# A spectral-mixing kernel on one core: features folded as well as tokens, with rows turned round through memory on ScalarE's queue

## The chip, the cores and the metric

The kernel runs on one core of a Trainium2 chip. The metric is the device time of one execution in microseconds (us); less is better. The five engines of a core are named as in the profile: PE (TensorE: matmuls, transposes; PEld is its weight load), DVE (VectorE), ACT (ScalarE), POOL (GpSimd) and SP (SyncE, which here only issues DMAs). Each engine works through its own instructions in a fixed order and waits for other engines and for DMAs by semaphores. All times of before are from one profiled execution unless a line says otherwise.

## The reference

Attention with a sigmoid in the place of a softmax, a real 2D Fourier transform with a residual, a layer norm and a feed-forward block with a second residual, in float32 on 8 batches of 448 tokens with 12 heads of 64 (768 features):

```python
scores = matmul(q, k.transpose(0, 1, 3, 2)) / sqrt(64) - log(448)
attn = matmul(1 / (1 + exp(-scores)), v)
x = attn.transpose(0, 2, 1, 3).reshape(8, 448, 768)

mixed = real(fft(fft(x, axis=1), axis=2))       # over tokens, then over features
u = x + mixed
mu = mean(u, -1); var = mean((u - mu) ** 2, -1)
un = (u - mu) / sqrt(var + 1e-6)
y = u + maximum(un @ w_ch1, 0) @ w_ch2          # 768 -> 3072 -> 768
```

## The kernel before

**Phases.** The first quarter of the span (to about 381 us) is attention and mixing, batch by batch. While it runs, the FFN's weights are read, split and combined in the background (`weight`, line 287: ACT L305, DVE L310 to L319, one weight block after another, with buffers `wr`, `wt`). After it the FFN runs: first token chunk 0 by plain products (PE `psh` L607 and `po` L627, while ACT, DVE and POOL make the weights for the fast form, L456, L458, L466), then the other chunks by a fast scheme (`psf` L845, `pso` L901).

**The attention loop.** The loop over `t` (line 567) goes in steps of two, one step being about 1.96 us on PE; 8 steps make a group of 4 heads and 24 steps a batch. In each pass PE makes scores (L139, L152), ACT the sigmoid `a` (L127) and the upper part `hi` of the next queries and keys (L115), DVE their remainder `lo` (L123), and PE the products with the values (`av`, L165 and L177), which ACT copies out as `xT` (L185): features on the partitions, 6 blocks of 128, and tokens along the row, folded already by even and odd halves (2 x 225). What else runs at a step is written down by hand with `at(t, fn)`; `pin` (line 503) then fixes each engine's order as emitted, so nothing is reordered later. An instruction that waits holds up all behind it on its engine.

**Mixing.** The transform over features is a matmul with cosines and sines (`stage_d`, PE `psd` L216), that over tokens a second one (`stage_s`, PE `pss` L227). Ahead of both, POOL folds `xT`: per feature pair p of three, sums and differences of blocks p and p+3 (`eo`, L197), then of even and odd token halves (`fd`, L200), then of tokens mirrored (`xp`, L203); 6 operations each, 18 per batch, in three rounds at steps 12 to 17, 20 to 25, and 28 and 29 of the batch (table FOLDS, line 32). `stage_d` is then 24 matmuls of 193 columns per batch (2 x 2 outputs, 2 parities, 3 pairs). ACT copies the result to `A` (L220); `stage_s` is 4 matmuls of 385 columns, with a copy `Q` on ACT (L231) and sum and difference `sm`, `df` on DVE (L236). PE transposes `xT` back (`psx`, L248), DVE adds (`u`, L255), SP stores `u` to `u_dram` (L263).

These units of batch b come in three chunks (`mix_some`, line 485), each ahead of a new group of heads: chunk 1 at step 24b+36 (two `psd` outputs, the first `pss`), chunk 2 at 24b+44 (the other two `psd`, three transposes), chunk 3 at 24b+52, which is step 28 of the next batch (two `pss`, the other five transposes). PE runs a chunk in one piece, so it waits there for ACT's `A` and `Q` and for DVE's `df` and `u`; a `u` also frees the PSUM bank that a later `pss`, `psx` or `av` needs. The units of the last batch run later, among the first products of the FFN (`mix_rest`, line 654).

**First norms.** The norm of chunk 0 (512 tokens, two groups of two 128-row tiles) is spread over steps too (`norm_plan`, line 430). From a group's start: load `un` at +4, statistics (DVE L373, L376) at +10, the inverse root by some ten tiny DVE operations on `mv` (L382 to L394) at +11, scaling `un` (DVE L399) at +17, the fp16 upper half `hl` (ACT L422) at +19 and +27, its remainder (DVE L426) and two transposing DMAs `ut<-hl` at +22 and +30. The groups start at steps 96 and 128.

Of the kernel before, what the change touches and what calls it, by code (L numbers as in the profile page):

```python
# [9 lines left out]
F32 = mybir.dt.float32  # L10
# [41 lines left out]
def spectral_attention_ffn(tc, qk, v, w1, w2, cd, cs, ident_in, out):  # L52
# [8 lines left out]
    with ExitStack() as top:  # L61
# [19 lines left out]
        if True:  # L81
# [87 lines left out]
            def values(gg, w):  # L169
                b, r = divmod(gg, NG)  # L170
                p = r + 3 * w
                vr, ps = vrs[gg], avs[gg][w]
                for c in range(3):
                    a = att.pop((2 * gg + w, c))
                    for j in range(2):
                        h = c * 256 + (2 * w + j) * D
                        nc.tensor.matmul(  # L177
                            ps[j * D:(j + 1) * D, :SQ], vr[:, h:h + D], a[:, j], start=False, stop=(c == 2))
# [6 lines left out]
                nc.scalar.activation(xT[:, p].rearrange("d r k -> d (r k)"), ps[:, :SQ], AF.Copy)  # L185

            eos = {}

            def fold(b, p, n, e):

                xT, xp = xts[b]
                lv, n = divmod(n, 2)
                op = (ALU.add, ALU.subtract)[n]
                if lv == 0:
                    if n == 0:
                        eos[p] = [fx.tile([128, 2, 2, HS], F32, tag=t, name=t) for t in ("eo", "fd")]
                    e.tensor_tensor(out=eos[p][0][:, n], in0=xT[:, p], in1=xT[:, p + 3], op=op)  # L197
                elif lv == 1:
                    eo, fd = eos[p]
                    e.tensor_tensor(out=fd[:, n], in0=eo[:, :, 0], in1=eo[:, :, 1], op=op)  # L200
                else:
                    fd = eos[p][1]
                    e.tensor_tensor(  # L203
                        out=xp[:, n, :, :, p], in0=fd[:, :, :, 0:HM], in1=fd[:, :, :, HS - 1:HM - 2:-1], op=op)

            def mix_units(b):
                xT, xp = xts[b]
                A = fx.tile([HM, 2, 2, 386], F32, tag="A", name="A")
                ps_d, sd, ut = {}, {}, {}

                def stage_d(kp, c, par, p):
                    m = HM - kp
                    if par == 0 and p == 0:
                        ps_d[c, kp] = ps_m.tile([128, 512], F32, tag="m", name="psd")
                    ps = ps_d[c, kp]
                    nc.tensor.matmul(  # L216
                        ps[:HM, par * 193:par * 193 + 193], xp[:, kp ^ c, c, par, p],
                        cd_sb[:, c, par, p], start=(p == 0), stop=(p == 2))
                    if par == 1 and p == 2:
                        act_next.append(lambda: nc.scalar.activation(  # L220
                            A[:, kp, c].rearrange("s (i r) -> s r i", r=2),
                            ps[:HM, 0:386].rearrange("s (r i) -> s r i", r=2), AF.Copy))

                def stage_s(kp, c):
                    m = HM - kp
                    ps = ps_m.tile([128, 512], F32, tag="m", name="pss")
                    nc.tensor.matmul(  # L227
                        ps[:m, :385], cs_sb[:HM, kp, c, :m], A[:, kp, c, :385], start=True, stop=True)
                    if c == 1:
                        sd["Q", kp] = Q = fx.tile([128, 385], F32, tag="Q", name="Q", bufs=2)  # L230
                        act_next.append(lambda: nc.scalar.activation(Q[:m], ps[:m, :385], AF.Copy))  # L231
                    else:
                        Q = sd["Q", kp]
                        sd[kp] = [fx.tile([128, 385], F32, tag=n, name=n) for n in ("sm", "df")]
                        for o, op in zip(sd[kp], (ALU.add, ALU.subtract)):
                            dve_next.append(lambda o=o, op=op: nc.vector.tensor_tensor(  # L236
                                out=o[:m], in0=ps[:m, :385], in1=Q[:m], op=op))

                def add_x(kp, r, hf):
# [6 lines left out]
                    ps = ps_m.tile([128, 512], F32, tag="m", name="psx")  # L246
                    for i in range(3):
                        nc.tensor.transpose(  # L248
                            ps[:HM - kp, i * 128:(i + 1) * 128], xT[:, hf * 3 + i, r, kp:HS:2], ident)
                    y = d if hf == r else s  # L250
                    m = HM - kp
                    ysl = y[:m, 384:0:-1] if hf else y[:m, 0:384]

                    def add():
                        nc.vector.tensor_tensor(  # L255
                            out=u[:m, hf * 384:hf * 384 + 384], in0=ps[:m, :384], in1=ysl, op=ALU.add)
                        if hf:
# [10 lines left out]
                def units_d(kp, c):  # L268
                    return [(0.33, lambda par=par, p=p: stage_d(kp, c, par, p)) for par in range(2) for p in range(3)]

# [58 lines left out]
            def weight_row():  # L329
# [3 lines left out]
                top = cpool.tile([128, 1], F32, name="top")  # L333
                row = cpool.tile([128, 128], F32, name="row")
                nc.vector.tensor_reduce(out=top[:2], in_=ps[:2, :128], op=ALU.max, axis=AX.X)
# [693 lines left out]
def _layout(q, k, v, w1, w2):  # L1029
    import numpy as np  # L1030
    B = q.shape[0]

    qt, kt = (a.reshape(B, 2, NG, 2, S, D).transpose(0, 2, 1, 3, 5, 4).reshape(B, 2 * NG, 2 * D, S) for a in (q, k))
# [60 lines left out]
```

## Time and profile before

| | |
|---|---|
| median of 3 runs | 1582.52 us (1581.5 to 1583.43) |
| the profiled execution's own time | 1581.96 us |
| its span (first to last instruction) | 1580.2 us |
| PE busy | 99% of the span |
| DVE busy | 81% |
| ACT busy | 42% |
| POOL busy | 20% |

The profile lists groups of instructions by source line. `out<-in` are the tiles written and read, followed by their shapes; `xN` is a count; then come busy time, the mean duration in ns, and idle time of that engine just before the group with whatever released it. A row of a timeline is: start in us, time taken, engine, line, operation, tiles, count, and in brackets the idle time before it and its releaser. A row of a table of stretches has the stretch (from:to), its length, and the busy time of PE, PEld, DVE, ACT and POOL with their instructions (x), the granted clock of PE (1.00 is full), the busy share of the 16 DMA engines, and GB/s.

### The profile page before, as it was taken

How to read it: one execution, taken by the hardware profiler on the slowest of the kernel's cores; microseconds unless marked ns; L12 is line 12 of the kernel's file. 1: busy time of each engine (PE TensorE's matmuls, PEld its weight loads, DVE VectorE, ACT ScalarE, POOL GpSimd, SP SyncE). 2: the span in 40 equal slices, each digit the busy share in tenths (PEclk: the TensorE clock that was granted, in tenths of full speed). 3: DMA queues.
4: the chain of work that ended last, by engine and by line, in shares of the span. 5: the costliest groups of instructions: out<-in, count | busy, mean ns of one | idle time of the engine just before them, and what ended most of it. 6: DMA issues, size and time to landing. Idle time of an engine off the chain costs nothing.

```text
span 1580.2 us, 27410 instructions
## 1 busy us (share of the span) xinstructions
PE 1557.3 (99%) x11059; PEld 1064.9 (67%) x11059; DVE 1277.1 (81%) x2354; ACT 656.4 (42%) x780; POOL 322.5 (20%) x244
## 2 busy tenths in 40 slices
PE   8999999899999999999999999999999999999998
PEld 3556565466555567777777777777777777777775
DVE  4997788794699946887888888888788878887778
ACT  7777777665555424222232233232423233223221
POOL 3644343355788810000000000000000000000000
PEclk9999999999999999999999999999999999999999
DMA  7888878783788977668667766866776777576571
GB/s 291 313 313 277 308 260 304 258 298 107 287 278 292 320 306 293 199 234 306 234 191 289 253 235 227 306 205 252 259 255 195 282 288 234 168 298 259 195 273 49
DMA packets 130399, 402.43 MB, mean 255 GB/s; under 512 B 68832, under 2 KB 70112, under 8 KB 111712
## 3 DMA queue, kind: packets, MB, share of 16 engines
q1 hardware_dynamic: 130272, 400.68, 71.1%
q8 instruction: 86, 1.41, 0.4%
q14 instruction: 41, 0.34, 0.1%
HBM read 311.39 MB, written 73.92 MB: 244 GB/s over the span
## 4 chain that ended last, share of the span: by engine, by line
PE 72%; DVE 3%; ACT 1%; issue 0%; DVEq 0%; ACTq 0%
PE pso L901 30%; PE psf L845 30%; PE psh L607 6%; PE po L627 5%; DVE F L851 1%; PE psd L216 0%; DVE H L851 0%; ACT H L880 0%; DVE ur L648 0%; DVE ur L929 0%; DVE acc L978 0%; DVE acc L916 0%; PE psx L248 0%; ACT F L870 0%; DVE X L851 0%
## 5 line engine op out<-in xcount | busy, mean ns | idle before, releaser
L845 PE MATMUL psf<-ut,ws 128*128 128x256 f16 x4536 | 506.6, 273 | 1.2 <-DVE ur L648 1.2
L901 PE MATMUL pso<-ws,H 128*128 128x384 f16 x3024 | 503.4, 326 | 1.1 <-DVE H L851 0.9
L845 PEld LDWEIGHTS <-ws 128*128 128x128 f16 x4536 | 443.6, 98 | 60.6 <-issue 1.7
L901 PEld LDWEIGHTS <-H 128*128 128x128 f16 x3024 | 295.5, 98 | 190.0 <-DVE H L851 1.7
L870 ACT ACTIVATE F<-F 128x1024 f32<-128x1024 f32 x72 | 76.1, 1057 | 406.5 <-DVE F L851 406.5
L916 DVE TENSOR_TENSOR acc<-pso,acc 128x384 f32<-128x384 f32 x399 | 207.9, 551 | 19.7 <-PE pso L901 19.7
L851 DVE TENSOR_TENSOR H<-F,H 128x1024 f16<-128x1024 f32 (+1 forms) x144 | 155.4, 1088 | 48.8 <-ACT H L880 48.5
L880 ACT ACTIVATE H<-F 128x1792 f16<-128x1792 f32 x72 | 122.2, 1697 | 110.7 <-DVE F L851 110.7
L127 ACT ACTIVATE a<-sc 128x900 f32<-128x900 f32 x168 | 147.2, 920 | 48.4 <-PE sc L139 47.7
L851 DVE TENSOR_TENSOR F<-X,psf 128x256 f32<-128x256 f32 x288 | 117.2, 419 | 59.3 <-PE psf L845 54.7
L466 POOL TENSOR_TENSOR wq<-wq 128x384 f32<-128x384 f32 x96 | 152.0, 1589 | 31.4 <-DVE wp L458 25.8
L851 DVE TENSOR_TENSOR F<-F 128x256 f32<-128x256 f32 x288 | 109.5, 422 | 24.8 <-ACT F L870 20.1
L177 PE MATMUL av<-a,vr 128*64 128x450 f32 x576 | 119.1, 550 | 0.0
L458 DVE SCALAR_TENSOR_TENSOR wp<-wq,wsc,wp 128x1536 f16<-128x1536 f32 x48 | 98.2, 2076 | 17.3 <-ACT wp L456 17.3
L851 DVE TENSOR_TENSOR X<-X,psf 128x256 f32<-128x256 f32 x216 | 89.9, 416 | 17.9 <-PE psf L845 16.3
L607 PE MATMUL psh<-ut,wp 128*128 128x512 f16 x432 | 98.5, 379 | 0.0
L197 POOL TENSOR_TENSOR eo<-xT 128x450 f32<-128x450 f32 x48 | 52.7, 1118 | 210.2 <-ACT xT L185 210.2
L859 ACT ACTIVATE X<-psf 128x256 f32<-128x256 f32 x72 | 27.8, 386 | 155.2 <-PE psf L845 155.2
L627 PE MATMUL po<-wp,hh 128*128 128x256 f16 (+1 forms) x384 | 88.6, 326 | 0.0
L177 PEld LDWEIGHTS av<-a,vr 128*64 128x64 f32 x576 | 37.2, 136 | 69.2 <-issue 69.2
L456 ACT ACTIVATE wp<-wq,wsc 128x1536 f16<-128x1536 f32 x48 | 73.5, 1570 | 23.3 <-DMA wq<-t_dram 20.8
L607 PEld LDWEIGHTS <-wp 128*128 128x128 f16 x432 | 42.2, 98 | 49.4 <-issue 0.8
(91 smaller groups left out, 1606.2 us busy)
## 6 DMA issues: line engine op xcount, KB each, us to landing
ws<-w_dram SPq DMA_DIRECT2D x144, 1344.0 KB, 7.4
wr<-w_in SPq DMA_DIRECT2D x48, 768.0 KB, 6.5
w_dram<-wp SPq DMA_DIRECT2D x24, 1344.0 KB, 7.8
qk<-qk_in SPq DMA_DIRECT2D x23, 898.0 KB, 7.8
t_dram<-wt SPq DMA_DIRECT2D x48, 384.0 KB, 6.4
wq<-t_dram SPq DMA_DIRECT2D x24, 768.0 KB, 6.0
vr<-v_in SPq DMA_DIRECT2D x24, 448.0 KB, 5.6
U<-u_dram SPq DMA_DIRECT2D x24, 384.0 KB, 9.1
```

What stands on the lines that cost most here:

```text
L127: nc.scalar.activation(a, ps[:, :, :SQ], AF.Sigmoid, bias=-math.log(S), scale=1.0 / math.sqrt(D))
L177: nc.tensor.matmul(ps[j * D:(j + 1) * D, :SQ], vr[:, h:h + D], a[:, j], start=False, stop=(c == 2))
L458: nc.vector.scalar_tensor_tensor(out=w[:, 1, part], in0=t, scalar=sc, in1=w[:, 0, part], op0=ALU.mult, op1=ALU.subtract)
L466: nc.gpsimd.tensor_tensor(out=t[:, o], in0=t[:, x], in1=t[:, y], op=op)
L607: nc.tensor.matmul(hs[c, f], l[:, m], r[:, m], start=(m == n == 0), stop=(m == NCC - 1 and n == 2))
L627: nc.tensor.matmul(po[n][:, at:at + hi - lo], l[:, cols], r[:, lo:hi], start=(f == 0 and m == 0 and at == 0), stop=(f == NFC - 1 and m == ...
L845: nc.tensor.matmul(ps[:, :TH], w[:, x, a, m * 128:(m + 1) * 128], ut[y][:, b, m], start=(m == n == 0), stop=(m == n == 2))
L851: nc.vector.tensor_tensor(out=o, in0=x, in1=y, op=op)
L870: nc.scalar.activation(F[:, 0:4], F[:, 0:4], AF.Relu)
L880: nc.scalar.activation(hts[P][:, 0], F[:, 1:8], AF.Copy)
L901: nc.tensor.matmul(ps[:, :384], H[:, x, a, tp * 128:(tp + 1) * 128], w[:, y, b], start=(j == n == 0 and half != 1), stop=(j == 1 and n == ...
L916: later(0, lambda: nc.vector.tensor_tensor(out=to, in0=ps[:, :384], in1=to, op=ALU.add))
```

## The change

**Folding over features, too.** A further fold level pairs the features once more: a feature and its mirror. With heads and columns reordered on the host (HEADS, `_columns`, the matrices in `_layout`), the mirror of a block lies in another block on the same partitions, except for a few features, whose rows must come to another partition. The fold over blocks p and p+3 and over token halves stays (levels 0 and 1; for p = 2 the result goes straight to the place of `xp`'s third part, `last`); then a level 2 adds and subtracts `fd` of blocks 0 and 1; level 3 mirrors tokens as before, for two parts where three were. 18 POOL operations per batch remain 18, but at other steps: 4 at 12 to 15, 4 at 20 and 21, 10 at 28 and 29.

**Rows through memory.** `turn_rows` moves one partition's row (partition 64, 1800 values, and partition 0 of one half, 900 values) out to a DRAM tile `turn` at step 24 of the batch, and back to the other places at step 28: four DMAs per batch, issued on ACT's queue.

**PE.** `stage_d` becomes 16 matmuls of 198 columns per batch, `stage_s` 4 of 396, `A` is copied out as it lies, and the transposes multiply by a permutation (`perm`, loaded at step 22) rather than the identity. Their number stays.

**Norm groups.** They start at steps 96 and 136; within a group `hl` comes at +23 and +39, its remainder and the transposes at +25 and +41.

**Last batch.** Of its ten folds at steps 28 and 29 the five differences go to DVE, the five sums stay on POOL.

**Else.** `weight_row` moves by two steps, and its `row` tile to another pool.

```diff
-FOLDS = ((12, 13, 14, 15, 16, 17), (20, 21, 22, 23, 24, 25), (28, 28, 28, 29, 29, 29))
+FOLDS = ((12, 0, 0), (13, 0, 1), (14, 0, 2), (15, 0, 3), (20, 1, 0), (20, 1, 1), (21, 1, 2), (21, 1, 3), 
+         (28, 2, 0), (28, 2, 1), (28, 2, 2), (28, 2, 3), (29, 0, 6), (29, 0, 7), (29, 2, 4), (29, 2, 5), (29, 2, 6), (29, 2, 7))
+NB = 66
+NL = 6 * NB
...
+        turn = dram.tile([2, 3, 4, HS], F32, name="turn")
...
-            cd_sb = c1.tile([128, 2, 2, 3, 193], F32, name="cd_sb")
+            cd_sb = c1.tile([128, 2, 2, 2, NL // 2], F32, name="cd_sb")
+            perm = c1.tile([128, 3, 128], F32, name="perm")
...
                 elif lv == 1:
-                    eo, fd = eos[p]
-                    e.tensor_tensor(out=fd[:, n], in0=eo[:, :, 0], in1=eo[:, :, 1], op=op)
+                    eo = eos[p]
+                    e.tensor_tensor(out=fd[:, 2 * n:2 * n + 2], in0=eo[:, :, 0], in1=eo[:, :, 1], op=op)
+                elif lv == 2:
+                    k = slice(1, 3) if n else slice(0, 4, 3)
+                    e.tensor_tensor(out=fd[:, k], in0=fd[:, k], in1=fds[b][:, 1, k], op=op)
                 else:
-                    fd = eos[p][1]
+                    fd = fd.rearrange("p (c r) n -> p c r n", c=2)
                     e.tensor_tensor(
-                        out=xp[:, n, :, :, p], in0=fd[:, :, :, 0:HM], in1=fd[:, :, :, HS - 1:HM - 2:-1], op=op)
+                        out=xp[:, n, :, :, 1 - p // 2], in0=fd[:, :, :, 0:HM], in1=fd[:, :, :, HS - 1:HM - 2:-1], op=op)
+
+            def turn_rows(b, back):
+
+                fd, tmp = fds[b], turn[b % 2]
+                pairs = ((fd[64:65], tmp[1:3] if back else tmp[0:2]), (fd[0:1, 1:2], tmp[0:1] if back else tmp[2:3]))
+                for x, y in pairs:
+                    x, y = x.rearrange("o a k n -> o (a k n)"), y.rearrange("(o a) k n -> o (a k n)", o=1)
+                    nc.scalar.dma_start(*((x, y) if back else (y, x)))
...
                     nc.tensor.matmul(
-                        ps[:HM, par * 193:par * 193 + 193], xp[:, kp ^ c, c, par, p],
-                        cd_sb[:, c, par, p], start=(p == 0), stop=(p == 2))
-                    if par == 1 and p == 2:
+                        ps[:HM, par * NL // 2:(par + 1) * NL // 2], xp[:, kp ^ c, c, par, p],
+                        cd_sb[:, c, par, p], start=(p == 0), stop=(p == 1))
+                    if par == 1 and p == 1:
                         act_next.append(lambda: nc.scalar.activation(
-                            A[:, kp, c].rearrange("s (i r) -> s r i", r=2),
-                            ps[:HM, 0:386].rearrange("s (r i) -> s r i", r=2), AF.Copy))
+                            A[:, kp, c], ps[:HM, 0:NL], AF.Copy))
...
-                    for n, t in ((1, 10), (7, 17), (8, 19 + 8 * j), (9, 22 + 8 * j)):
+                    for n, t in ((1, 10), (7, 17), (8, 23 + 16 * j), (9, 25 + 16 * j)):
...
-                for r, when in enumerate(FOLDS):
-                    for n, t in enumerate(when):
-                        at(24 * b + t, lambda b=b, r=r, n=n: fold(b, r, n, nc.gpsimd))
+                for t, p, n in FOLDS:
+                    e = nc.vector if b == B - 1 and t > 27 and n % 2 else nc.gpsimd
+                    at(24 * b + t, lambda b=b, p=p, n=n, e=e: fold(b, p, n, e))
+                for k, t in enumerate((24, 28)):
+                    at(24 * b + t, lambda b=b, k=k: turn_rows(b, k))
...
-            at(TP + 2, weight_row)
+            at(TP + 4, weight_row)
...
-                        at(96 + 32 * g + n, fn)
+                        at(96 + 40 * g + n, fn)
```

The order of the instructions shows where these land. ACT's rows at steps 72 to 77, the end of batch 2's attention, before (`a` are sigmoids, `hi` the next head pair's upper parts, `Q` belongs to chunk 3 of the batch ahead):

```order
L127 ACTIVATE a<-sc 128x900
L185 ACTIVATE xT<-av 128x450
L127 ACTIVATE a<-sc 128x900 x2
L305 ACTIVATE wt<-wr 128x768
L185 ACTIVATE xT<-av 128x450
L127 ACTIVATE a<-sc 128x900 x2
L115 ACTIVATE hi<-qk 128x898
L231 ACTIVATE Q<-pss 112x385
```

The same place on ACT now:

```order
L133 ACTIVATE a<-sc 128x900
L225 DMA turn<-fd 1x1800
L225 DMA turn<-fd 1x900
L192 ACTIVATE xT<-av 128x450
L133 ACTIVATE a<-sc 128x900 x2
L326 ACTIVATE wt<-wr 128x768
L192 ACTIVATE xT<-av 128x450
L133 ACTIVATE a<-sc 128x900 x2
L225 DMA fd<-turn 1x1800
L225 DMA fd<-turn 1x900
L121 ACTIVATE hi<-qk 128x898
L251 ACTIVATE Q<-pss 112x396
```

The rows go out behind the group's half-width sigmoid, and come back behind the two sigmoids of step 28, ahead of `hi` and of the `Q` for which chunk 3 waits.

On DVE, the statistics of the second norm group (`stt`, `mv`) before, where they stood ahead of the additions of batch 4's chunk 2 (`u`):

```order
L319 SCALAR_TENSOR_TENSOR wt<-wr,wt 128x768
L373 BN_STATS stt<-un 128x6 x2
L376 BN_AGGR mv<-stt 128x2
...
L391 TENSOR_TENSOR mv<-mv 128x2
L392 SCALAR_TENSOR_TENSOR mv<-mv 128x2
L394 SCALAR_TENSOR_TENSOR mv<-mv 128x2
L255 TENSOR_TENSOR u<-psx,df 113x384
L255 TENSOR_TENSOR u<-psx,sm 113x384 x2
L123 TENSOR_TENSOR lo<-qk,hi 128x898
```

And now, eight steps later, ahead of that batch's chunk 3 (`u`, then `sm` and `df` of its second half):

```order
L340 SCALAR_TENSOR_TENSOR wt<-wr,wt 128x768
L394 BN_STATS stt<-un 128x6 x2
L397 BN_AGGR mv<-stt 128x2
...
L412 TENSOR_TENSOR mv<-mv 128x2
L413 SCALAR_TENSOR_TENSOR mv<-mv 128x2
L415 SCALAR_TENSOR_TENSOR mv<-mv 128x2
L277 TENSOR_TENSOR u<-psx,df 113x384
L256 TENSOR_TENSOR sm<-pss,Q 112x396
L256 TENSOR_TENSOR df<-pss,Q 112x396
```

The 16 operations are the same; they moved from ahead of a chunk's first additions to ahead of a chunk in which PE waits for `df`.

Last, DVE at step 196, where attention ends. Before, the row ahead of chunk 3 of batch 6 was one weight product (`wp`):

```order
L255 TENSOR_TENSOR u<-psx,sm 113x384 x2
L458 SCALAR_TENSOR_TENSOR wp_3726<-wq,wsc,wp_3726 128x1536
L255 TENSOR_TENSOR u<-psx,df 113x384
L236 TENSOR_TENSOR sm<-pss,Q 112x385
L236 TENSOR_TENSOR df<-pss,Q 112x385
```

Now five folds of batch 7 stand between them (`eo`, `xp` and `fd` are the fold tiles; POOL has the same five shapes of its own at this place):

```order
L479 SCALAR_TENSOR_TENSOR wp_3685<-wq,wsc,wp_3685 128x1536
L207 TENSOR_TENSOR eo<-xT 128x450
L210 TENSOR_TENSOR xp<-eo 128x450
L216 TENSOR_TENSOR xp<-fd 128x4x113
L213 TENSOR_TENSOR xp<-xp,fd 128x450
L216 TENSOR_TENSOR xp<-xp 128x4x113
L277 TENSOR_TENSOR u<-psx,df 113x384
L256 TENSOR_TENSOR sm<-pss,Q 112x396
L256 TENSOR_TENSOR df<-pss,Q 112x396
```

DVE's share of batch 7's folds comes ahead of all that chunk 3 of batch 6 wants from it.

More of the change, by code (lines that the diff above doesn't have):

```diff
@@ L26 @@
 CP = 128
+HEADS = [0, 5, 4, 3, 1, 2, 6, 11, 10, 9, 7, 8]
 CH = 64
@@ L246, in add_x @@
                     ps = ps_m.tile([128, 512], F32, tag="m", name="psx")
-                    for i in range(3):
+                    for i, (j, n) in enumerate((((0, 0), (1, 0), (2, 0)), ((3, 1), (5, 2), (4, 2)))[hf]):
                         nc.tensor.transpose(
-                            ps[:HM - kp, i * 128:(i + 1) * 128], xT[:, hf * 3 + i, r, kp:HS:2], ident)
-                    y = d if hf == r else s
+                            ps[:HM - kp, i * 128:(i + 1) * 128], xT[:, j, r, kp:HS:2], perm[:, n])
                     m = HM - kp
-                    ysl = y[:m, 384:0:-1] if hf else y[:m, 0:384]
+                    y = (d if hf == r else s)[:m].rearrange("s (r b k) -> s b r k", r=2, k=NB)
+                    y = y[..., 0:64] if hf else y[..., 2:66]
                     def add():
-                        nc.vector.tensor_tensor(
-                            out=u[:m, hf * 384:hf * 384 + 384], in0=ps[:m, :384], in1=ysl, op=ALU.add)
+                        o, x = (t.rearrange("s (b r k) -> s b r k", r=2, k=64)
+                                for t in (u[:m, hf * 384:hf * 384 + 384], ps[:m, :384]))
+                        nc.vector.tensor_tensor(out=o, in0=x, in1=y, op=ALU.add)
                         if hf:
@@ L268, in units_d @@
                 def units_d(kp, c):
-                    return [(0.33, lambda par=par, p=p: stage_d(kp, c, par, p)) for par in range(2) for p in range(3)]
+                    return [(0.33, lambda par=par, p=p: stage_d(kp, c, par, p)) for par in range(2) for p in range(2)]
                 def units_s(kp, c):
@@ L333, in weight_row @@
                 top = cpool.tile([128, 1], F32, name="top")
-                row = cpool.tile([128, 128], F32, name="row")
+                row = fx.tile([128, DM], F32, tag="w5", name="wt")[:, :128]
                 nc.vector.tensor_reduce(out=top[:2], in_=ps[:2, :128], op=ALU.max, axis=AX.X)
@@ L543, in spectral_attention_ffn @@
             at(17, lambda: nc.sync.dma_start(cd_sb, cd))
-            at(22, lambda: (nc.sync.dma_start(cs_sb, cs), nc.sync.dma_start(ident, ident_in)))
+            at(22, lambda: (nc.sync.dma_start(cs_sb, cs), nc.sync.dma_start(ident, ident_in[:, 0]),
+                            nc.sync.dma_start(perm, ident_in[:, 1:])))
             ends = sorted([(t, (-10, -5, -1, 0, 3)) for t in range(15, TP, 8)]
@@ L1031, in _layout @@
     B = q.shape[0]
+    q, k, v = (a[:, HEADS] for a in (q, k, v))
+    v = v.copy()
+    for h in (2, 3, 8, 9):
+        v[:, h] = v[:, h][..., -np.arange(D) % D]
+    w1, w2 = w1[_columns()], w2[:, _columns()]
     qt, kt = (a.reshape(B, 2, NG, 2, S, D).transpose(0, 2, 1, 3, 5, 4).reshape(B, 2 * NG, 2 * D, S) for a in (q, k))
@@ L1043, in _layout @@
     w2t = np.ascontiguousarray(w2.reshape(NFC, 128, DM).transpose(1, 0, 2)).reshape(128, -1).view(np.int64)
-    cd = np.zeros((128, 2, 2, 3, 193), np.float32)
-    d = np.arange(384).reshape(3, 128)
+    cd = np.zeros((128, 2, 2, 2, NL // 2), np.float32)
+    r = np.arange(64)
+    d = np.stack([np.arange(64, 192), np.concatenate([r, [192], 321 + r[:63]])], axis=1)
+    h, places = _heads(), _places()
+    order = [np.concatenate([a for b, m in enumerate((1, 2, 2)) for a in (
+        384 - h[-b % 3][places[m, k, :2]], h[b][places[0, k]])]) for k in range(2)]
     for par in range(2):
-        l = np.arange(par, 385, 2)
+        l = order[par]
         ang = (d[:, :, None] * l) % 768
@@ L1052, in _layout @@
                 m[(ang % 384) == 0] = 0.0
-            cd[:, c, par, :, :len(l)] = m.transpose(1, 0, 2)
+            cd[:, c, par] = m
     n = n[:HM]
@@ L1064, in _layout, with _heads, _places, _columns @@
     return {"qk_in": qk, "v_in": vt, "w1_in": w1t, "w2_in": w2t, "cd_in": cd, "cs_in": cs,
-            "id_in": np.eye(128, dtype=np.float32)}
+            "id_in": np.stack([np.eye(128, dtype=np.float32)] + [
+                np.eye(128, dtype=np.float32)[:, p.ravel()] for p in _places()], axis=1)}
+def _heads():
+    import numpy as np
+    r = np.arange(64)
+    p = np.arange(128)
+    return np.stack([np.concatenate([r, 320 + r]), np.where(p % 64, 320 - p, 256 - p), 64 + p])
+def _places():
+    import numpy as np
+    res = np.zeros((3, 2, 64), int)
+    for k in range(2):
+        core = np.array([n for n in range(2, 128) if n % 64 > 1 and n % 2 == k])
+        ends = np.array([k, 64 + k])
+        res[0, k] = np.concatenate([core, ends])
+        res[1, k] = np.concatenate([(128 - ends) % 128 if k else ends, 128 - core])
+        res[2, k] = np.concatenate([ends, core])
+    return res
+def _columns():
+    import numpy as np
+    l, p = _heads(), _places()
+    half = [l[b][p[0].ravel()] for b in range(3)]
+    return np.concatenate(half + [384 + l[b][p[n].ravel()] for b, n in ((0, 1), (2, 2), (1, 2))])
 def _tokens():
@@ L1091 @@
     res = np.empty_like(y)
-    res[:, _tokens()] = y
+    res[:, _tokens()[:, None], _columns()] = y
     return res
```

30 lines of the change are left out of this document (17 added, 13 removed).

## The prediction

> **What bounds the kernel now.** The page's first lines come first: which engine is busy.
>
> ```profile
> PE 1557.3 (99%) x11059; PEld 1064.9 (67%) x11059; DVE 1277.1 (81%) x2354; ACT 656.4 (42%) x780; POOL 322.5 (20%) x244
> ```
>
> PE has hardly a gap, so PE work that goes is time, and a new wait of PE is time too. The change touches only the first 390 us, so the second view is a table of stretches there, cut where chunk 1 of a batch begins on PE (five of eight; the columns are explained above):
>
> ```profile
> core 0: us, PE busy (x) PEld busy (x) DVE busy (x) ACT busy (x) POOL busy (x), PEclk, DMA share, GB/s
> 58.18:105.29 47.11, 46.61 (x311) 27.79 (x309) 43.94 (x59) 34.72 (x47) 23.74 (x19) 1.00 0.82 291
> 152.39:199.47 47.08, 46.59 (x310) 27.79 (x308) 37.55 (x55) 34.23 (x46) 19.41 (x19) 1.00 0.86 319
> 199.47:247.33 47.86, 46.84 (x310) 27.91 (x308) 41.88 (x70) 35.26 (x48) 21.46 (x19) 1.00 0.85 276
> 247.33:299.65 52.32, 49.27 (x310) 28.78 (x308) 43.16 (x73) 34.84 (x46) 17.81 (x18) 0.97 0.73 251
> 299.65:349.08 49.43, 46.88 (x311) 27.86 (x309) 42.31 (x58) 36.09 (x49) 22.92 (x19) 1.00 0.90 315
> ```
>
> A plain batch takes 47.1 us, nearly all PE. Three batches with norm work take 0.8, 5.2 and 2.3 more. The third view is the timeline in the last two of these:
>
> ```profile
> 281.62 0.84 ACT L422 ACTIVATE hl<-un 128x768 f16<-128x768 f32 x1 [2.79 <-DVE un L399]
> 285.79 0.59 PE L248 MATMUL psx<-ident,xT 128*112 128x128 f32 x3 [1.93 <-ACT Q L231]
> ...
> 301.72 0.84 ACT L422 ACTIVATE hl<-un 128x768 f16<-128x768 f32 x1 [3.81 <-DMA ut<-hl]
> 305.91 0.90 PE L227 MATMUL pss<-A,cs_sb 113*113 113x385 f32 x2 [2.07 <-ACT A L220]
> ```
>
> ACT stands at `hl`, first for DVE's scaling, then for the transposing DMAs that still read the buffer; `xT`, `a`, `hi`, `Q` or `A` queue behind, and PE waits for them. The clock adds to it:
>
> ```profile
> 284.00:287.30 3.30, 1.04 (x6) 0.78 (x6) 1.42 (x3) 1.74 (x3) 3.14 (x4) 0.99 1.01 413
> 287.30:290.70 3.40, 3.40 (x18) 2.12 (x20) 3.40 (x6) 1.48 (x2) 1.77 (x2) 0.50 0.13 54
> ```
>
> After 3.3 us in which PE was busy for 1.04, it ran 3.4 us at half clock: 1.7 us lost.
>
> **The change part by part.** (1) PE's matmuls. Priced from the chain of waits (a matmul of float32 leaves two records there):
>
> ```profile
> 385.48 1.97 PE psd L216 x12
> 390.70 0.65 PE pss L227 x2
> ```
>
> 12 records are 6 matmuls: 1.97/6 = 0.328 us for 193 columns, 1.70 ns a column. `pss` with 385 columns takes 0.655 by the same price, so there is no fixed part. 198 columns give 0.337, 396 give 0.674. Per batch: 24 x 0.328 = 7.88 goes, 16 x 0.337 = 5.39 comes, and 4 x 0.019 = 0.08 on `pss`: -2.42. Eight batches: **-19.3**. The transposes keep their count and size, the matrix they multiply with has no price.
>
> (2) Norm waits that go. `hl` now follows its scaling by 6 steps where it was 2, and the second `hl` follows the first's transposes by 14 where it was 5. At 1.96 us a step that covers waits of 2.79 and 3.81, so the 5.2 and 2.3 go: **-7.5**. The 0.8 of the stretch at 199 stays: group 0's statistics keep their step.
>
> (3) DMA issues on ACT. Two stand ahead of `hi` and `Q` in chunk 3 of batches 0 to 5. No row shows ACT issuing a DMA; SP's issue is the nearest.
>
> ```profile
> 136.52 0.38 SPq L104 DMA_DIRECT2D qk<-qk_in  x1
> 138.59 0.95 ACT L115 ACTIVATE hi<-qk 128x898 fp32r<-128x898 f32 x1
> 141.04 0.59 PE L248 MATMUL psx<-ident,xT 128*112 128x128 f32 x3 [0.47 <-DVE df L236]
> ```
>
> PE already waits 0.47 for `df` there, so a delay of ACT passes through: up to 2 x 0.38 in six batches, 4.6; nothing if the issue goes out while the sigmoids ahead still run. I take **+1**, near the lower end, as no row has the engine itself standing for an issue. The way out, at step 24, lies ahead of nothing urgent.
>
> (4) POOL's ten folds at steps 28 and 29, where six were. The first `psd` needs the last of them.
>
> ```profile
> 136.73 1.92 POOL L197 TENSOR_TENSOR eo<-xT 128x450 f32<-128x450 f32 x2 [9.52 <-ACT xT L185]
> 138.73 1.91 POOL L200 TENSOR_TENSOR fd<-eo 128x450 f32<-128x450 f32 x2
> 140.72 2.09 POOL L203 TENSOR_TENSOR xp<-fd 128x452 f32<-128x452 f32 x2
> 152.39 0.91 PE L216 MATMUL psd<-cd_sb,xp 128*113 128x193 f32 x4
> ...
> 45.66 2.24 POOL L197 TENSOR_TENSOR eo<-xT 128x450 f32<-128x450 f32 x2 [2.55 <-ACT xT L185]
> 47.97 3.23 POOL L200 TENSOR_TENSOR fd<-eo 128x450 f32<-128x450 f32 x2
> 51.28 2.83 POOL L203 TENSOR_TENSOR xp<-fd 128x452 f32<-128x452 f32 x2
> 58.18 4.19 PE L216 MATMUL psd<-cd_sb,xp 128*113 128x193 f32 x24
> ```
>
> In a plain batch four operations end at 140.6; then POOL waits for the rows. They are issued about when ACT's sigmoids end, 138.7. The nearest row for a small DMA is this:
>
> ```profile
> u_dram<-u SPq DMA_DIRECT2D x8, 45.0 KB, 4.8
> ```
>
> So rows at 143.5, then six operations of 1.05 to 1.5: 149.8 to 152.5. PE wants them at 152.4: hidden, barely. Batch 0 has contended operations and an earlier `psd`: four to 51.2, six by 1.42 to 59.7, 1.5 late: **+1.5** (0 to 4).
>
> (5) Statistics ahead of chunk 3 at step 148. Their price stands at the first group:
>
> ```profile
> 198.97 1.01 DVE L373 BATCH_NORM_STATS2 stt<-un 128x6 f32<-128x384 f32 x2
> 203.09 0.90 DVE L391 TENSOR_TENSOR mv<-mv 128x2 f32<-128x2 f32 x1
> 206.22 0.16 DVE L394 SCALAR_TENSOR_TENSOR mv<-mv 128x2 f32<-128x2 f32 x1
> ...
> 138.69 0.56 DVE L255 TENSOR_TENSOR u<-psx,df 113x384 f32<-113x384 f32 x1 [2.24 <-PE psx L248]
> ```
>
> 7.4 us from 198.97 to 206.4, of which some 3 are tiny operations at 0.90 beside POOL's folds that take 0.16 without. In chunk 3 DVE has 2.24 idle ahead of `u`. A chain of 7.4 makes `u` 5.2 and `df` 4.4 late (0.7 of idle after `u` takes the rest); one of 4.4 makes `df` 1.4 late. POOL works through the first half of it: about 3 late. Bounds 1.4 and 4.4 + 1.7 of half clock; I take **+4**. Two remainders of `hl` come nearer to chunk 2 of batch 5: **+1** (0 to 3).
>
> (6) The last batch's folds on DVE, ahead of chunk 3 of batch 6.
>
> ```profile
> 378.06 0.55 ACT L185 ACTIVATE xT<-av 128x450 f32<-128x450 f32 x1 [1.72 <-PE av L177]
> 379.22 0.56 DVE L255 TENSOR_TENSOR u<-psx,df 113x384 f32<-113x384 f32 x1 [2.27 <-PE psx L248]
> 381.00 0.59 PE L248 MATMUL psx<-ident,xT 128*112 128x128 f32 x3 [0.19 <-DVE df L236]
> ...
> L774 DVE TENSOR_TENSOR U<-U 128x384 f32<-128x384 f32 x40 | 21.3, 554 | 0.3
> L736 DVE TENSOR_TENSOR U<-U 128x384 f32<-128x384 f32 x8 | 7.2, 944 | 0.2
> ```
>
> `xT` ends at 378.6 and starts both engines. A DVE fold takes 0.65 (0.554 by 450/384; 944 is the same operation beside POOL's work), a POOL fold 0.96 (1.92 for two). If they run by turns, as these rows and the tiny operations of (5) suggest, five pairs cost 5 x 1.6 = 8.0; then `u`, `sm`, `df` take 1.6: `df` at about 387.5, the last transposes 6.6 later than 381.0. Side by side POOL's five set the pace, 4.8 us, and DVE waits for it at level 2: 4.7 late. All work of PE behind, the FFN's first product included, is queued behind these transposes, so nothing covers it, and PE stands for over 3.4 us, which may bring the half clock of above (1.7). **+8.3** (4.7 to 10, with POOL's weight sums later too).
>
> The Trainium skill's page "SBUF — State Buffer", section "Who interferes with whom", says that a VectorE operation with two SBUF inputs and a GpSimd operation that reads SBUF exclude each other for the whole instruction. The rows agree: 0.90 against 0.16 with and without POOL. By it the folds run by turns and the sum is the one above; without it 1.9 less.
>
> The page "TensorE: Matmul & The Clock Gate", Part 1, has the clock halve after an idle window of about 3.4 us. Here a window with 1.04 us of work in it was enough, so the trace is harsher than the rule. By the rule (6) may cost 6.6, and the sum be 1.7 lower.
>
> (7) DMA. A plain batch at 44.7 us with the bytes of 47.1 has a share of 0.91 (0.86 x 47.08/44.7); the stretch at 299.65 would need 0.90 x 49.43 = 44.5 of 44.7. Loads can then come late: **+1** (0 to 3).
>
> **Sum.** -19.3 - 7.5 + 1 + 1.5 + 4 + 1 + 8.3 + 1 = -10.0. The profiled execution took 1581.96 (its span of 1580.2 and 1.8 around it), 0.6 below the median: 1581.96 - 10.0 = **1572.0**.
>
> **The rivals.** *The rows come late* (slower). If the way back takes not 4.8 us but 8, as bulk loads nearly do, POOL resumes at 146.7 and ends at 153.0 to 155.7, and PE stands 0.6 to 3.3 us at each `psd` of seven batches. It decides from about 6 us on; at 2 us a batch it adds 14: 1586. For it: the DMA share of 0.82 to 0.90, and two waits for memory in a row. Against it: few bytes, and 45 KB landed in 4.8.
>
> *The new waits are small*: with (3), (4), (7) at nothing and (5), (6) at their lower ends, 1581.96 - 26.8 + 6.1 = 1561.3. For it: ACT and POOL do have slack in plain batches. Against it: the rows of (5) and (6) show the chains in full.
>
> *The gain doesn't come off* since DVE or DMA sets the pace: DVE is busy 43.94 in the first stretch and 43.16 and 42.31 in the norm's, against a new period of 44.7, where every wait counts. Were each of three stretches held at 47, -7.3 of the -19.3 goes: 1579.3, and with somewhat larger stalls 1581: no change that shows.
>
> **How the numbers follow.** Forecast 0.70, small waits 0.10, gain held 0.09, late rows 0.11. A measurement of this kernel tells some 0.2% (3.2 us) from no change. Of the forecast's 0.70, 0.66 is faster by more than that and the rest the same; the rival of small waits is faster; half of the held gain is the same, a little faster; late rows are slower, with a small share the same. Faster 0.78, same 0.11, slower 0.11. All costs at their upper ends (4.6, 4, 6.1, 3, 10, 3) give 1585.9, all at the lower 1561.3: range 1562 to 1585.
>
> **What would show it.** In the profile after: plain periods of about 44.7 us between chunks 1; no wait of `hl` for `ut`; PE idle of some 3 us before `psx` in batch 4's chunk 3, ended by `df`; PE idle of 5 to 7 us before the last attention transposes, and 3.4 us of half clock behind it; batch 0's `psd` behind POOL by 1 to 2 us. It is wrong if PE waits for `xp` in every batch (the rows), if plain periods stay near 47, or if DVE's folds end before 384.

## The result and the profile after

The changed kernel took 1599.57 us (median of 4 runs, 1598.87 to 1599.9) against 1582.97 of the kernel before in the same comparison: a ratio of 1.0109, 95% interval 1.0097 to 1.0121. It is slower by 17 us where the prediction had 10 us less and its range ended at 1585. The profiled execution took 1599.35, its span 1597.6, so 17.4 us more than the one of before.

The page's first lines, then the table of stretches between first `psd` matmuls of batches, as shown for before (columns as there):

```profile
span 1597.6 us, 27182 instructions
PE 1551.1 (97%) x10931; PEld 1050.5 (66%) x10931; DVE 1295.9 (81%) x2359; ACT 655.3 (41%) x780; POOL 331.3 (21%) x239
```

```profile
61.92:109.70 47.78, 46.16 (x293) 26.73 (x293) 37.77 (x49) 33.28 (x45) 23.14 (x19) 0.96 0.66 226
109.70:156.34 46.64, 44.71 (x293) 25.30 (x293) 41.74 (x54) 34.55 (x47) 23.20 (x19) 1.00 0.85 297
156.34:202.32 45.98, 44.71 (x293) 25.23 (x293) 41.87 (x54) 33.85 (x46) 24.94 (x19) 1.00 0.93 345
202.32:255.62 53.30, 47.61 (x293) 26.53 (x293) 48.34 (x72) 34.46 (x46) 25.68 (x19) 0.94 0.73 244
255.62:306.77 51.15, 46.56 (x295) 26.78 (x293) 43.53 (x68) 35.25 (x48) 22.18 (x19) 0.93 0.71 257
306.77:360.83 54.06, 48.48 (x295) 26.86 (x293) 48.48 (x63) 35.88 (x49) 23.25 (x19) 0.94 0.80 278
```

PE has 6 us less work than before over the whole span, though its matmuls run slowly for a while, and still the span is longer. Even the two undisturbed-looking stretches are 46.6 and 46.0, not 44.7, and four of six show a granted clock below 1.

Where PE stood is in its timeline. These are its rows with an idle time of over 2 us in the first 430 us, and one of 0.88 for its releaser:

```profile
61.92 4.62 PE L237 MATMUL psd<-cd_sb,xp 128*113 128x198 f32 x16 [3.84 <-POOL xp L216]
...
96.74 0.59 PE L268 MATMUL psx<-perm,xT 128*112 128x128 f32 x3 [0.88 <-ACT Q L251]
...
241.53 0.90 PE L268 MATMUL psx<-perm,xT 128*112 128x128 f32 x3 [3.07 <-ACT Q L251]
...
292.42 2.18 PE L268 MATMUL psx<-perm,xT 128*112 128x128 f32 x9 [3.65 <-DVE u L277]
...
327.63 0.59 PE L268 MATMUL psx<-perm,xT 128*113 128x128 f32 x3 [2.26 <-ACT A L241]
...
346.83 0.59 PE L268 MATMUL psx<-perm,xT 128*112 128x128 f32 x3 [2.61 <-ACT Q L251]
...
395.79 1.85 PE L268 MATMUL psx<-perm,xT 128*112 128x128 f32 x6 [5.50 <-DVE u L277]
```

Three releasers, then: POOL's last fold in batch 0; DVE at the statistics (292) and at the last batch's folds (396); and, not foreseen in this size, ACT's `Q` and `A`. ACT's timeline shows what held it (an idle time before `hi`, `xT` or `wt`, with what ended it; ACTq is ACT's sequencer, which issues DMAs):

```profile
94.71 0.54 ACTq L225 DMA_DIRECT2D fd<-turn  x2
95.34 0.95 ACT L121 ACTIVATE hi<-qk 128x898 fp32r<-128x898 f32 x1 [0.78 <-DMA fd<-turn]
...
234.76 0.20 ACTq L225 DMA_DIRECT2D fd<-turn  x1
239.89 0.20 ACTq L225 DMA_DIRECT2D fd<-turn  x1
240.14 0.95 ACT L121 ACTIVATE hi<-qk 128x898 fp32r<-128x898 f32 x1 [4.34 <-DMA ut<-hl]
...
280.52 2.90 ACTq L225 DMA_DIRECT2D turn<-fd  x2
283.46 0.55 ACT L192 ACTIVATE xT<-av 128x450 f32<-128x450 f32 x1 [3.76 <-DMA un<-u_dram]
...
323.34 0.95 ACT L326 ACTIVATE wt<-wr 128x768 f32<-128x768 f32 x1 [3.26 <-DMA wr<-w_in]
...
336.53 2.03 ACTq L225 DMA_DIRECT2D turn<-fd  x2
338.61 0.55 ACT L192 ACTIVATE xT<-av 128x450 f32<-128x450 f32 x1 [4.03 <-DMA t_dram<-wt]
345.44 0.95 ACT L121 ACTIVATE hi<-qk 128x898 fp32r<-128x898 f32 x1 [1.79 <-DMA wr<-w_in]
```

The issue itself costs 0.20 us and runs beside a sigmoid. But at 234.76 one row DMA goes out and the other only at 239.89, just after a transposing DMA of the norm has landed, with which it shares no data. The built program says why: the DMAs of SP and ACT take turns on the same eight semaphores, and one goes out only when the last on its semaphore has landed. The order of ACT's rows with their waits, at that place:

```
L225 DMA fd<-turn 1x1800 [waits DMAHW3_49,DMAHW2_49]
L225 DMA fd<-turn 1x900 [waits DMAHW4_49]
```

The second row waits for semaphore 4 alone, whose last user is `ut<-hl`, issued by SP at 237.38. ACT stands in its own queue for SP's DMA; `hi` and `Q` are behind it, and PE is behind `Q`.

The clock is the other surprise. Stretches of 3.4 us around three of the gaps:

```profile
236.40:239.80 3.40, 0.95 (x7) 0.56 (x5) 1.42 (x2) 0.00 (x0) 3.32 (x4) 0.99 0.29 69
239.80:243.20 3.40, 1.49 (x6) 0.98 (x6) 1.60 (x4) 1.34 (x2) 1.36 (x2) 0.50 1.04 300
243.20:246.60 3.40, 3.40 (x18) 2.12 (x20) 3.37 (x8) 1.35 (x2) 2.15 (x1) 0.50 0.92 341
...
325.30:328.70 3.40, 1.14 (x8) 0.93 (x9) 3.37 (x3) 2.66 (x5) 3.32 (x3) 0.97 0.26 58
328.70:332.10 3.40, 3.40 (x16) 1.68 (x18) 3.37 (x5) 2.42 (x3) 1.71 (x2) 0.53 1.02 285
...
345.80:349.20 3.40, 1.88 (x12) 1.52 (x14) 2.29 (x5) 0.98 (x2) 2.36 (x3) 0.97 1.00 410
349.20:352.60 3.40, 3.40 (x20) 1.50 (x22) 3.37 (x6) 2.81 (x4) 3.17 (x3) 0.53 0.76 266
```

A gap of 2.3 to 2.6 us was enough for 3.4 us at half clock, one of 3.1 had 6.8. Such stretches add up to some 31 us, against 3.4 before. PE was busy for some 25 of them, so about 12 us were lost to the clock alone, 10.7 more than before. Together with 22 us more of idle time between matmuls (32 against 10, summed over PE's timeline from 20 to 400 and 420 us) that outweighs the 19.3 us of matmuls saved, by 13. The other 4 of the 17.4 us are 1.6 of idle time later in the span and some 2.4 of PE's busy time that this sum does not explain.

A gap's length alone does not settle what the clock does. In every trace here the clock changes on a grid of 3.41 us. Two runs that are told below, each cut on its own grid: the rows on SP, and all folds of the last batch on POOL.

```profile
243.68:247.09 3.41, 1.63 (x7) 0.97 (x6) 0.00 (x0) 2.79 (x5) 3.33 (x4) 1.00 1.02 402
247.09:250.50 3.41, 3.41 (x18) 1.86 (x16) 2.41 (x4) 0.98 (x2) 0.13 (x1) 0.50 1.03 417
...
397.14:400.55 3.41, 1.64 (x8) 0.55 (x6) 0.69 (x1) 0.60 (x1) 3.25 (x4) 1.00 0.36 121
400.55:403.96 3.41, 1.50 (x9) 1.50 (x10) 0.00 (x0) 0.00 (x0) 3.33 (x4) 1.00 0.00 0
403.96:407.38 3.42, 3.42 (x19) 2.40 (x17) 0.00 (x0) 2.73 (x3) 3.26 (x4) 1.00 0.00 0
```

A gap of 1.78 us that lay in one window was followed by half clock, one of 3.69 us that fell into two was not. Over all 14 traces, from 20 to 440 us, every full-clock window with less than 1.5 us of PE work was followed by half clock and none with more than 1.7 us was; between these it went both ways.

### The profile page after: what moved, and what is told of

Its sections match the earlier page's. It is cut to its first block, busy times and chain, and to the rows that moved or that the text cites. A ratio compares the mean times of both kernels' runs of the same rounds, so it can differ in the third digit from the quotient of the medians.

```text
span 1597.6 us, 27182 instructions
## 1 busy us (share of the span) xinstructions
PE 1551.1 (97%) x10931; PEld 1050.5 (66%) x10931; DVE 1295.9 (81%) x2359; ACT 655.3 (41%) x780; POOL 331.3 (21%) x239
## 4 chain that ended last, share of the span: by engine, by line
PE 72%; DVE 7%; DMA 2%; issue 1%; ACT 1%; POOL 1%; SPq 0%; ACTq 0%; DVEq 0%; POOLq 0%
PE psf L869 29%; PE pso L925 29%; PE po L651 4%; PE psh L631 4%; PE av L183 2%; PE sc L145 1%; DVE wp L479 1%; PE psd L237 1%; DMA ws<-w_dram 1%; DMA U<-u_dram 1%; DVE wt L338 1%; DVE F L875 1%; POOL wq L487 1%; DVE lo L129 1%; DVE wt L331 1%
## 5 line engine op out<-in xcount | busy, mean ns | idle before, releaser
L487 POOL TENSOR_TENSOR wq<-wq 128x384 f32<-128x384 f32 x96 | 148.7, 1555 | 39.4 <-DVE wp L479 23.5
L207 POOL TENSOR_TENSOR eo<-xT 128x450 f32<-128x450 f32 x47 | 54.6, 1182 | 193.1 <-ACT xT L192 193.1
L129 DVE TENSOR_TENSOR lo<-qk,hi 128x898 fp32r<-128x898 f32 (+2 forms) x50 | 59.0, 1184 | 21.0 <-ACT hi L121 20.9
```

Source lines behind the costliest of these rows:

```text
L487: nc.gpsimd.tensor_tensor(out=t[:, o], in0=t[:, x], in1=t[:, y], op=op)
```

## The experiments

Each ratio is to the kernel before in the same comparison; the changed kernel stands at 1.0109.

### What the rows cost

**Without the rows:**

```diff
-                for k, t in enumerate((24, 28)):
-                    at(24 * b + t, lambda b=b, k=k: turn_rows(b, k))
```

> Leaves out the four row DMAs per batch, so a few rows of the transform are not moved and are wrong. Theory Q (ACT stands at its row DMAs until an unrelated DMA on the same semaphore has landed, PE stands behind ACT's Q, and SP's loads come later because each DMA waits for the one eight issues before): the stalls of ACT at 93, 240, 283, 338 and 345 us go, with the half clock behind them, and the waits of ACT for wr shrink: 1580 to 1587 us, with no wait of ACT for a DMA ahead of hi or xT. Rival F (the folds, the statistics and the last batch cost the time, the rows are an onlooker): 1595 to 1600 us, with the same gaps of PE.

1584.89 us, 1.0013 (1.0004 to 1.0023). Theory Q: 15 of the 17 us hang on four small DMAs per batch. PE's gap at batch 0's `psd` was 1.26 in the place of 3.84, and ACT had no wait for a DMA ahead of `hi` and `xT`. The gap at the statistics, however, had grown from 3.65 to 8.95: POOL no longer pauses for the rows and folds beside the whole chain. PE's two rows without the rows and, below them, POOL's pause in the changed kernel:

```profile
59.43 2.77 PE L237 MATMUL psd<-cd_sb,xp 128*113 128x198 f32 x15 [1.26 <-POOL xp L216]
...
285.48 2.18 PE L268 MATMUL psx<-perm,xT 128*112 128x128 f32 x9 [8.95 <-DVE u L277]
```

```profile
293.84 3.45 POOL L216 TENSOR_TENSOR xp<-fd 128x452 f32<-128x452 f32 x2 [2.94 <-DMA fd<-turn]
```

**The rows issued by POOL,** at steps 22 and 26, on semaphores that only POOL's DMAs use:

```diff
-                    nc.scalar.dma_start(*((x, y) if back else (y, x)))
+                    nc.gpsimd.dma_start(*((x, y) if back else (y, x)))
...
-                for k, t in enumerate((24, 28)):
+                for k, t in enumerate((22, 26)):
```

> Same computation; the row DMAs are issued by POOL at steps 22 and 26, on semaphores of their own. Theory Q: like the run without rows, 1580 to 1588 us, since nothing of ACT or SP waits for them. Rival R (the round trip through memory itself is what POOL and PE wait for, whoever issues it): POOL still stands before its first mirrored fold, batch 0 is as late as now, and the time is 1592 us or more. Rival F: 1595 to 1600.

1590.13, 1.0048 (1.0032 to 1.0065): 9.5 us better, between the two expectations. ACT's waits for DMAs ahead of `hi` and `xT` were gone, but batch 0 was as late as in the changed kernel, since POOL stood for the way out and spent 1.0 us on the issue before its folds:

```profile
45.96 1.03 POOL L225 DMA_DIRECT2D fd<-turn  x2 [5.92 <-DMA turn<-fd]
47.00 1.93 POOL L207 TENSOR_TENSOR eo<-xT 128x450 f32<-128x450 f32 x2
```

**The rows issued by SP,** at the same steps, on the shared semaphores (`nc.sync` in the place of `nc.scalar`):

> Same computation; the row DMAs are issued by SP at steps 22 and 26, on the semaphores that they share with all of SP's DMAs. Theory Q (what costs is mostly that ACT stands at the issue): ACT has no wait for a DMA ahead of hi or xT, SP's loads are as late as in the changed kernel, and the time is 1588 to 1595 us. Rival Q2 (what costs is that the rows take turns on the shared semaphores and make SP's loads late): 1596 us or more, with longer waits of ACT for wr.

1585.28, 1.0017 (1.0008 to 1.0027), as good as without the rows at all and below the 1588 at which theory Q's range began. So the sharing of semaphores doesn't cost much where nothing of PE's chain is queued behind the DMA.

**The control: still on ACT, at steps 22 and 26:**

> Same computation; the row DMAs stay on ACT but at steps 22 and 26, the steps of the runs with POOL and SP. A control: theory Q (it is the engine that issues them) says ACT still stands at them for other DMAs, at other places, 1592 us or more; if the steps alone made the runs on POOL and SP faster, the time is 1584 to 1588 us and ACT has no wait for a DMA ahead of hi or xT.

1589.33, 1.0042 (1.0026 to 1.0058): below the 1592 that theory Q named, so the steps alone bring 10 us. There the rows are back before POOL needs them, batch 0's gap falls from 3.84 to 1.27, and behind the DMAs stands `hi` of a later group, not chunk 3's `Q`. ACT still stands, and PE with it, at three places for 0.9, 2.4 and 2.5 us:

```profile
323.38 3.89 ACTq L225 DMA_DIRECT2D turn<-fd  x2
327.32 0.95 ACT L121 ACTIVATE hi<-qk 128x898 fp32r<-128x898 f32 x1 [5.71 <-DMA qk<-qk_in]
```

Four of the 17 us thus go with the engine, ten with the place in its queue and the time that it leaves the rows to land. Rows on another engine at the old steps 24 and 28 were not run, so what the engine alone brings there is open.

### What the norm's steps are worth

**The old norm steps in the changed kernel:**

```diff
-                    for n, t in ((1, 10), (7, 17), (8, 23 + 16 * j), (9, 25 + 16 * j)):
+                    for n, t in ((1, 10), (7, 17), (8, 19 + 8 * j), (9, 22 + 8 * j)):
...
-                        at(96 + 40 * g + n, fn)
+                        at(96 + 32 * g + n, fn)
```

> Same computation; the norm groups are 32 steps apart, with hl and its remainder at their old steps. Theory N (old waits of hl come back, 7.5 us, the new stall of 3.7 us at the statistics and its 2 us of half clock go, and the wait of ACT's row DMA for the transposes at 240 us goes elsewhere): within 4 us of the changed kernel, 1596 to 1603. Rival: the new steps were the whole loss at 240 and 292 us and the time falls by 8 or more, to 1591 or less.

1600.64, 1.0118 (1.0103 to 1.0133): the same within the intervals. `hl` again waited 5.1 and 2.8 us for `un` and 4.0 for `ut`, the gap at the statistics went.

**The new norm steps alone, in the kernel before** (the same lines the other way):

> The kernel before with the new norm steps alone (groups 40 apart, hl at 23 and 39). Theory D: the waits of hl for un and ut go, 7.5 us and 1.7 of half clock, and the statistics, which now stand ahead of chunk 3 beside POOL's folds, cost PE 5 to 9 us there: 1579 to 1585 us. Rival: the spacing of the groups is a gain by itself and the statistics fit into DVE's idle time: 1573 to 1577.

1582.95, 1.0003 (0.9993 to 1.0012): no difference. The 7.5 us that the prediction credited came: five of the six stretches between batches took 47.1 to 47.8. The fifth took 54.6, and one gap in it, with its half clock, took all of the gain back:

```profile
286.48 2.18 PE L248 MATMUL psx<-ident,xT 128*112 128x128 f32 x9 [6.06 <-DVE u L255]
```

**Group 1 at step 140** (`96 + 44 * g`, with the rows on POOL):

> Same computation; the rows on POOL as before, and norm group 1 starts at step 140 in the place of 136, so its statistics stand behind chunk 3 of batch 4, not ahead of it. Theory D (DVE's statistics, slowed by POOL's folds that no longer pause for the rows, hold up u and df of that chunk for 9 us with half clock behind): PE's gap before psx near 290 us goes and the time is 1576 to 1581 us, against 1590 of the rows on POOL. Rival: the chain only moves and holds up the next lo or df as long: 1587 us or more.

1588.02, 1.0035 (1.0022 to 1.0049), 2 us better than the rows on POOL, which the intervals don't tell apart, where theory D had 9 to 14. The gap of 9.1 us at chunk 3 was gone, but the chain, now four steps later and in part still beside POOL's folds, held up `lo`, and PE for 4.66 us. The rival was right: it only moved.

**Group 1 at step 132,** with the rows on SP, so that the statistics run where POOL has no folds:

```diff
-                    for n, t in ((1, 10), (7, 17), (8, 23 + 16 * j), (9, 25 + 16 * j)):
+                    for n, t in ((1, 10), (7, 17), (8, 23 + 12 * j), (9, 25 + 12 * j)):
...
-                        at(96 + 40 * g + n, fn)
+                        at(96 + 36 * g + n, fn)
```

> Same computation; rows on SP as in that run, and norm group 1 starts at step 132 (hl at 23 and 35, its remainder at 25 and 37), so that its statistics stand at steps 142 and 143, where POOL has no fold. Theory D: the chain takes some 5 us rather than 8 to 12 and falls between two chunks; the gap of 8.6 us at 285 us and 3 us of its half clock go: 1573 to 1578 us against 1585. Rival: it holds up the next lo or u there too: 1582 us or more.

1582.53, 1.0001 (0.9991 to 1.001): 2.8 us less than with the rows on SP, not 7 to 12: the rival's range. The chain did shrink. DVE's timeline of the rows on POOL (statistics beside folds) and, below it, of the second-to-last kernel of this study, which has the steps of this one:

```profile
277.51 1.01 DVE L394 BATCH_NORM_STATS2 stt<-un 128x6 f32<-128x384 f32 x2
...
282.95 0.90 DVE L413 SCALAR_TENSOR_TENSOR mv<-mv 128x2 f32<-128x2 f32 x1
...
288.42 0.91 DVE L415 SCALAR_TENSOR_TENSOR mv<-mv 128x2 f32<-128x2 f32 x1
```

```profile
270.16 0.16 DVE L403 TENSOR_SCALAR mv<-mv 128x2 f32<-128x2 f32 x1
...
272.33 0.16 DVE L415 SCALAR_TENSOR_TENSOR mv<-mv 128x2 f32<-128x2 f32 x1
...
277.40 1.62 DVE L340 SCALAR_TENSOR_TENSOR wt<-wr,wt 128x768 int32<-128x768 int32 x1
278.94 2.75 DVE L420 TENSOR_SCALAR un<-un,mv 128x768 f32<-128x768 f32 x2
```

The twelve tiny operations took 9.4 us beside POOL and 2.3 without. What held up chunk 3 now was the next in DVE's queue: the weights' operations, up to 1.62 rather than 0.96 each, and the scaling, 2.75 rather than 1.26 for two, all beside POOL's folds. PE still stood 5.8 us there.

### The last batch, and a version that is faster

**All folds of the last batch on POOL:**

```diff
-                    e = nc.vector if b == B - 1 and t > 27 and n % 2 else nc.gpsimd
+                    e = nc.gpsimd
```

> Same computation; POOL makes all folds of the last batch. Theory S (DVE's five folds hold up df of chunk 3 of batch 6, and PE at half clock behind it): PE's gap of 5.5 us before the last psx goes with 3 us of half clock, and the time is 1590 to 1593 us. Rival P (POOL's ten folds then end some 5 us later and the weight sums behind them hold up the FFN's first products as much): 1598 to 1601 us.

1598.29, 1.01 (1.0085 to 1.0115): 1.3 us less than the changed kernel, the same within the intervals, and on the side of rival P. The gap of 5.5 before the last `psx` went, and a new one of 3.69 us stood behind the first `psh`, at `psd`, which waited for POOL's tenth fold.

**A first combination:** rows on POOL, group 1 at step 140, one fold of batch 0 on DVE at step 33, and of the last batch three folds on DVE at step 198, behind its work for chunk 3:

```diff
-                    e = nc.vector if b == B - 1 and t > 27 and n % 2 else nc.gpsimd
+                    e = nc.gpsimd
+                    if b == B - 1 and (p, n) in ((0, 7), (2, 5), (2, 6), (2, 7)):
+                        t = 30
+                        e = nc.gpsimd if n == 6 else nc.vector
+                    if b == 0 and (p, n) == (0, 7):
+                        t, e = 33, nc.vector
```

> Same computation; rows on POOL, group 1 at step 140, and of the last batch's folds three go to DVE at step 198, behind DVE's work for chunk 3 of batch 6; one fold of batch 0 goes to DVE at step 33. If the stalls found add up (1590 of the rows on POOL, 11 to 13 for the statistics, some 4 of the last batch, 1.5 of batch 0): 1571 to 1576 us, faster than both kernels. Rival: POOL's end of the last folds holds up psd and the weight sums as in the run without a share, and batch 0 gains nothing: 1577 us or more.

1583.97, 1.0009 (0.9999 to 1.0019): the rival's range, not the 1571 to 1576 hoped for, by the `lo` that the statistics held up (4.65 us here) and by batch 0 (2.69). The last batch worked: no gap before the last `psx`, and 1.5 us at `psd`.

**The second:** rows on SP, group 1 at step 132, the three late folds:

> The run before (rows on SP, statistics at 142) with three folds of the last batch on DVE at step 198, behind DVE's work for chunk 3 of batch 6. Theory S: another 3 to 5 us off, 1569 to 1575 us, faster than both kernels. Rival P: POOL's later end holds up psd and the weight sums as much as it gains: within 1.5 us of the run before.

1578.53 (1575.98 to 1580.44), 0.9974 (0.9964 to 0.9984): faster than both kernels, and 4 us better than without the late folds, as theory S said, though not by as much as the sum had it. Its stretches, first and fifth:

```profile
59.34:103.97 44.63, 44.02 (x292) 25.28 (x292) 41.85 (x54) 34.02 (x47) 24.43 (x20) 1.00 0.80 281
...
241.22:296.13 54.91, 46.37 (x292) 26.55 (x292) 46.06 (x77) 37.70 (x51) 22.88 (x20) 0.94 0.83 286
```

Plain batches are at 44.6 to 44.8, the saving in full; most of what is left stands in the fifth.

**The third,** with the scaling of `un` one step later (`(7, 18)`), behind chunk 3:

> The run before with the scaling of un one step later (18 in the place of 17), which puts it behind chunk 3 of batch 4. Theory D (what DVE does ahead of that chunk beside POOL's folds is what PE waits for): the gap of PE there, 5.8 us in the run with the statistics at 142, falls below 3 us, with 2 to 3 us of half clock gone: 1572 to 1576 us. Rival: the weights ahead of it, slowed by POOL too, hold it up as long: 1577 to 1580.

1577.94, 0.997 (0.996 to 0.9981), no different from the second and in the rival's range, though not by the rival's cause: PE's gap at chunk 3 fell from 5.79 to 3.12, just short of the 3 expected, and another of 2.26, behind a load `wr` for which ACT waited 4.07, opened 35 us later, with 3.4 us of half clock.

## Why the prediction was wrong

**Step 3 failed, ACT's DMA issues.** It priced the issue, "up to 2 x 0.38 in six batches", bounded it by nothing and 4.6 us and took +1. The issue was nearly free; the wait in front of it was not. It took the DMA for an instruction with a duration where it was a wait: for the way out to land, and for whichever DMA last used its semaphore. Nothing in the first trace shows that price for ACT, but the built program's order, read with its waits, lists DMA semaphores on the row DMAs, and what was queued behind them, `hi` and `Q`, the step did name. Nor did the way out lie "ahead of nothing urgent": ACT stood idle for 3.8 and 4.0 us there, ahead of `xT` at 283 and 339. Leaving the rows out gave back 15 us, moving them ahead on ACT 10, moving them to SP 14.

**Step 4 was mis-sized for the same reason.** In plain batches the folds ended when PE wanted them, as forecast: in batches 1 to 3 PE waited 0.25 us each at `psd`. In batch 0 +1.5 became 3.84 us of idle time and 3.4 us at half clock: POOL waited 1.4 us for the rows, and its contended folds took 1.5 to 1.7, not 1.42. The step's 4.8 us for a row was somewhat short: where POOL issued them, rows took 5.0 to 5.8 in the median from issue to landing, each way. With the rows ahead of time, or left out, the gap is 1.26, the size forecast. The slower rival had this mechanism in every batch; it came in one.

**The clock was under-counted.** 1.7 us was added in two places, for the stalls of steps 5 and 6. Six stalls paid it, two of them behind gaps of 2.3 and 2.6, and three of them had twice the time at half clock.

**Step 1 was right:** chunks 1 and 2 were 1.20 and 1.25 us shorter wherever nothing disturbed them (2.42 per batch with 0.04 given back in chunk 3), and plain periods came to 44.6 to 45.0 in the runs with the rows on SP.

**Step 2 was right in itself and netted nothing with step 5:** -7.5 came (no `hl` waits in the profile after), and the statistics ahead of chunk 3 took it back, as the new steps alone in the kernel before show. (There even the 0.8 of the stretch at 199, which was to stay, went.) Step 5's +4 became 3.65 us of idle time and 6.8 us at half clock, in which PE was busy for 5.4 and so lost 2.7: 6.3 in all, just above the step's upper bound of 6.1. Without POOL's pause for the rows the idle time alone is 9. The +1 for the two remainders shows as no gap of PE.

**Step 6 was right:** 5.50 us of idle time against 6.6, with half clock behind. (Its terms, 378.6 + 8.0 + 1.6, add up to 388.2 for `df`, 0.7 above the 387.5 that it goes on with.) DVE's and POOL's folds did run by turns in part: POOL's took 1.1 to 1.5 us beside DVE's, 0.96 alone. That the other way is little better, because POOL's end then holds up `psd`, was not weighed.

**Step 7 was too small:** late `wr` loads held ACT for 2.8, 2.1 and 3.3 us and PE for 1.2, 0.5 and 2.3 behind `A`, 4 us in the place of 1. They came in the faster kernels too, where periods are shorter. In the run without the rows ACT waited 2.7, 3.1 and 2.3 us for `wr` as well, so the rows' turns on the semaphores are not needed for them; that the shorter period causes them was not shown.

**The rule on shared ports and the rule on the clock.** The first (the Trainium skill, "SBUF — State Buffer", "Who interferes with whom") agrees with 9.4 against 2.3 us for the same twelve operations, though three of the twelve have one tensor input, and two of these were stretched as well, to 0.90 and 1.00 us, which the rule as told above does not cover. The second ("TensorE: Matmul & The Clock Gate", Part 1) asks for an idle window of about 3.4 us, and windows with up to 1.7 us of work in them were followed by half clock here; the measurement decides.

## What to carry to other kernels

A DMA issued by a computing engine is a wait in that engine's queue: list what the DMA waits for, semaphores shared with other queues included, and what stands behind it. Give small round trips through memory to an engine behind which nothing urgent waits, several steps ahead of their use. And count a stall of PE at two prices, its length and the half clock behind it: in these traces half clock came wherever the idle time left less than 1.5 us of work in one window of the clock's grid of 3.41 us, at 1.7 us of loss for each such window that PE then worked through. Gaps of 1.8 to 2.4 us brought it in some places and not in others.

## What the runs showed of the hardware that was not expected

Half clock after windows in which PE had worked for nearly half of the time (up to 1.69 of 3.41 us), and none after two windows that shared a gap of 3.69 us. Two-element operations of DVE that stretch from 0.16 to 0.8 to 1.06 us beside POOL's folds, the ones with a single tensor input (`TENSOR_SCALAR`, 1.00 at the rows on POOL) among them. And that taking the rows away made another stall longer, 3.65 to 8.95 us, because POOL's wait for them (2.94 us) had kept POOL out of DVE's way.
